# Five shared PSUM banks, more heads in plain F32, and fewer transfers in a fused attention and gated-MLP kernel

## The chip, the cores and the metric

The kernel runs on one core of a Trainium2 chip. Each time is device time in microseconds (us) of one execution. The kernel before was timed three times: 784.73, 786.86 and 790.17 us; the median is 786.86 us. The profile comes from one further execution, which took 793.39 us.

A core has five engines that run side by side and wait for each other through semaphores: TensorE (PE in the profile; its weight loads are a row of their own, PEld), VectorE (DVE), ScalarE (ACT), GpSimd (POOL) and SyncE (SP), which in this kernel issues all the DMAs. TensorE writes into PSUM, eight banks of 128 x 512 F32 values; all else lies in SBUF.

## The reference

Two stages follow each other, for 8 batches of 576 positions. The first is attention with 8 heads of 64 dimensions per batch (64 heads in all); the second is a feed-forward part with a token-mixing gate, which adds its input at the end.

```python
scores = scale * np.matmul(q, k.transpose(0, 1, 3, 2))
cum = np.cumsum(np.maximum(s, 0.0), axis=-1)
bias = -(cum[:, :, :, None] - cum[:, :, None, :])
scores = np.where(causal, -1e9, scores + np.minimum(bias, 0.0))
attn = softmax(scores)                       # max taken off, sum + 1e-9
x = heads_side_by_side(np.matmul(attn, v))   # (8, 576, 512)

h = gelu_tanh(x @ w_in)                      # 512 -> 1024
u, v = h[..., :512], h[..., 512:]
v_n = (v - mean(v)) / np.sqrt(var(v) + 1e-6) * g_ln
v_s = np.einsum('ts,bsd->btd', w_sg, v_n) + b_sg[None, :, None]   # mixes positions
out = x + (u * v_s) @ w_out
```

In each row of scores the term of the query's own running sum is a constant, so only the key's running sum is added: a row of the running sum stands beside the key's 64 rows, and a row of ones beside the query's.

## The kernel before, in words

**Two ways to multiply.** TensorE takes plain F32, or F32R, a shortened F32. Most products are made in F32R from split operands: a value is copied as F32R (the high part), what is lost is taken off (`x - high`, the low part), and the products high x high, high x low and low x high are summed in PSUM. `split` (lines 590-597) makes the two parts, most often the high one on ACT and the low one on POOL or DVE. The first heads avoid splits: up to `NQ` (8) the scores, and up to `NP` (12) the sums of probabilities and values, are plain F32 products. In the profile an F32 product has two records.

**Scores of one head** (`scores`, lines 852-881). The 576 queries are five tiles, the keys are only taken up to the diagonal, so six products of 448, 64, 320, 192, 288 and 288 columns fill four PSUM banks. `qk_part` (799-807) makes one product in F32, or two in F32R. DVE adds the causal mask and finds the row's extreme (`ttr`), ACT takes the exponential and its sum (`exp_`). A scores bank is free again when DVE has read it. `transposes` (883-944) turns the probabilities on TensorE and copies or splits them out of PSUM; `pv` (946-1013) multiplies them with V. Every second head, `scales` and `spread_scales` send the inverse sums through DRAM and a broadcast.

**Operands of a head.** `load` (609-629) fetches a plain head's key and query as two blocks of 128 rows (64 of data, one of ones, 63 of zeros) and then puts the running sum in row 64 of the key's block. For a later head it fetches one raw block; `split_head` (781-797) splits it and moves the halves about with four SBUF copies and one transfer from DRAM (`k<-cum`). The first copy of a running-sum row (head 0) is also the gate behind which the loads under `later()` are issued: the weights of the feed-forward part and the raw blocks.

**Feed-forward part of one batch** (`ffn`, lines 1016-1160): 5 units `v` (into `vm`), 8 units `u` (`um`), 8 units `s` (`sm`, token mixing with the bias) and 8 units `o` (`om`), each with 8 to 14 products in one PSUM bank, followed by a series on ACT, DVE and POOL. It runs beside the attention of the next batch. The weights are prepared once, during the first two batches: `w_in` and `w_out` by a series on ACT, POOL and DVE per piece (`part`), the token weights by `w_sg_part` (744-769) from half tiles `wst` in the eight-buffer ring `u2`. The token bias goes as high and low part into rows 64 and 65 of `wr2`, by transfers.

**PSUM.** Four pools: scores two banks (`ps_sc`, line 582), transposes two, sums one, feed-forward three (`ps_m`, line 585). In the last batch, the feed-forward part draws on all but the sums' bank in turn (`rings`, line 1019). A pool's banks are given to its tiles in the order in which the tiles are written in the program.

**The order of the work.** The program is not written in the order in which it runs. Each step is placed at a time counted in heads (`POS`, `place`, `spread`), and each instruction gets that time as its priority, shifted by a table `SHIFT` per kind of instruction and phase. `plan` (437-560) then goes through a model of the engines with costs (`cost`, the table `FULL` for plain F32 products, `MARGIN`, `ISSUE`) and fixes for every engine the sequence in which it takes its instructions. Each engine runs its sequence strictly in that order. Eight products that nobody reads (`WARM`, tile `wm`, lines 656-658) stand before the first head.

All instructions go through one helper, so the profile has them all on line 418; groups are told apart by the names of their tiles.

Of the kernel before, what the change touches and what calls it, by code (L numbers as in the profile page):

```python
# [71 lines left out]
MARGIN = 54.24  # L72
ISSUE = 550.0
PHASE = (4.0, 9.0, 13.5, 61.5)
SHIFT = {
    "act activation p__ 128x192 p__": (3.011, -1.887, 0, 0, 0),
    "act activation p__ 128x576 p__": (-3.548, 0, 0, 0, 0),
# [3 lines left out]
    "act activation wbits 128x256 wraw": (-0.436, -0.436, -0.436, -0.436, 0),  # L81
    "act copy k 128x576 raw": (0, 4.274, 4.274, 4.274, 4.274),
    "act copy pah 128x512 pt": (0, 0, 1.072, 4.27, 0),
    "act copy pal 128x512 pt": (0, 0, 4.218, 0, 0),
    "act copy pbh 128x256 pt": (2.434, 2.434, 2.434, 2.434, 2.434),
    "act copy pbl 128x256 pt": (1.753, 1.753, 1.753, 0, 0),
    "act copy vs 128x384 vr": (0, 0, 1.645, 0, 0),
    "act copy wi 128x256 wbits": (1.607, 0, 0, 0, 0),
# [9 lines left out]
    "dve scalar_tensor_tensor wbits 128x256 wraw": (1.384, 1.384, 1.384, 1.384, 0),  # L98
    "dve scalar_tensor_tensor wm 128x256 wraw": (11.665, 0, 0, 0, 0),
    "dve tensor_copy pbl 128x512 pt": (2.602, 2.602, 2.602, 0, 0),  # L100
    "dve tensor_scalar wm 128x256 wbits": (-1.597, 3.567, 0, 0, 0),
    "dve tensor_tensor pbl 128x512 pt": (0, 0, 0, 5.115, 0),
    "dve tensor_tensor_reduce p__ 128x192 sc": (0, 0, 3.283, 0, 0),
    "dve tensor_tensor_reduce p__ 128x288 sc": (-1.373, 0, 0, 0, 0),
    "dve tensor_tensor_reduce p__ 128x320 sc": (6.772, 0, 6.985, 5.285, 0),
    "dve tensor_tensor_reduce p__ 128x448 sc": (-0.88, 0, 0, 0, 0),
    "dve tensor_tensor_reduce p__ 64x64 sc": (-11.268, -11.268, -11.268, -11.268, -11.268),
# [25 lines left out]
    "pool tensor_scalar p__ 64x64 p__": (0, 2.769, 0, 0, 0),  # L133
    "pool tensor_scalar wbits 128x256 wbits": (0, -2.08, 0, 0, 0),
    "pool tensor_tensor bh 1x288 wst": (0, 0, 4.905, 0, 0),
    "pool tensor_tensor vn 128x512 vt": (0, 0, -3.713, -3.713, -3.713),
    "pool tensor_tensor wo 128x256 wbits": (0, 0, 10.618, 10.618, 0),
    "pool tensor_tensor ws 128x288 wst": (0, 0, -1.463, 0, 0),
# [425 lines left out]
def tile_attn_gmlp(  # L564
    ctx: ExitStack,
    tc: tile.TileContext,
    kq: bass.AP,
    vp: bass.AP,
# [40 lines left out]
    def load(h):  # L609
        d = heads[h] = {}  # L610
        if h < NQ:
            k = d["k"] = att.tile([P, S], F32, name="kf", tag="k1")
            q = d["q"] = att.tile([P, S], F32, name="qf", tag="q1")
            nc.sync.dma_start(out=k, in_=kq[h, 0:P])
            nc.sync.dma_start(out=q, in_=kq[h, D:D + P])
            x = nc.sync.dma_start(out=k[D:D + 1, :], in_=cf[h:h + 1, :])
            if h == 0:
                first.append(x)
        else:
            d["raw"] = att.tile([P, S], F32, name="raw", tag="raw", bufs=1)  # L620
# [123 lines left out]
    def w_sg_part():  # L744
        with later():
            nc.sync.dma_start(out=g_b, in_=g_ln.rearrange("(o d) -> o d", o=1).broadcast_to([P, DH]))
        for j in range(NT):
# [7 lines left out]
        for f in range(2):
            fs = slice(f * CH, f * CH + CH)
            t = moe.tile([P, CH], F32, name="wst", tag="u2", bufs=U2)
            nc.sync.dma_start(out=t[0:REM, :], in_=w_sgt[NT * P:S, fs])
            nc.sync.dma_start(out=t[REM:P, :], in_=w_sgt[NT * P:S, fs])
            nc.scalar.copy(out=wr1[:, fs], in_=t)  # L760
# [508 lines left out]
```

## Time and profile before

| | |
|---|---|
| median of three executions | 786.86 us (784.73 to 790.17) |
| the profiled execution | 793.39 us, of which 791.7 us from the first to the last instruction |
| TensorE busy | 770.2 us (97%) |
| weight loads busy | 693.9 us (88%) |
| DVE, ACT, POOL busy | 602.8, 569.0, 497.6 us |
| data moved by DMA | 98.93 MB in 75567 packets |
| mean granted TensorE clock | 0.989 |

A row of the groups reads: line, engine, operation, output tile <- input tiles, the shape of one, its count | the time in which at least one of them ran (us), the mean of one (ns) | idle time of the engine before them and what ended it. A row of the stretches gives, from A to B us, the stretch's length, each engine's busy time with its count of instructions, the granted clock of TensorE as a share of full speed, and the DMA engines' busy share and GB/s. A row of the waits: engine and tile that waited <- engine and tile that ended it: us in total, times, longest. A row of the chain or of the timeline: start, length, what. TensorE's records overlap, since a matmul's record lasts from its issue to the end of its last result.

### The profile page before, as it was taken

To read this page: it belongs to the slowest core of one execution; us is meant where nothing else is said; L and a number is where in the kernel's file an instruction comes from. 1 tells how busy PE (TensorE), PEld (TensorE's weight loads), DVE (VectorE), ACT (ScalarE), POOL (GpSimd) and SP (SyncE) were. 2 spreads that over 40 slices of the span, in tenths; PEclk is the share of its full clock that TensorE was granted. 3 is DMA by queue.
4 is the path that set the end of the run, shared out by engine and by line. 5 is a ranking of instruction groups with operands and counts; after the bars stand their busy time and mean duration, and the time that the engine had idled before them with its cause. 6 is when DMAs were issued, how large, how long until landed. Compare 5 with 4: busy or idle time off the path is not lost.

```text
span 791.7 us, 16950 instructions
## 1 busy us (share of the span) xinstructions
PE 770.2 (97%) x5225; PEld 693.9 (88%) x5225; DVE 602.8 (76%) x1849; ACT 569.0 (72%) x1576; POOL 497.6 (63%) x775
## 2 busy tenths in 40 slices
PE   7999899999999999999999999999999999999998
PEld 5566667999989998999999998999989999999998
DVE  5884678877797688976798767976889767984562
ACT  4786667977688677886788776886788867882340
POOL 4588777667577566675566575775576756663632
PEclk9999889999999999999999999999999999999999
DMA  7777653465535553555444635355544555310101
GB/s 219 206 228 189 186 125 97 120 165 131 142 84 142 131 140 102 133 133 140 131 119 104 165 94 141 91 138 132 142 110 117 135 147 131 95 33 31 59 8 61
DMA packets 75567, 98.93 MB, mean 125 GB/s; under 512 B 27298, under 2 KB 43876, under 8 KB 75476
## 3 DMA queue, kind: packets, MB, share of 16 engines
q1 hardware_dynamic: 75476, 97.84, 46.3%
q8 instruction: 42, 0.69, 0.4%
q14 instruction: 49, 0.40, 0.2%
HBM read 51.71 MB, written 9.90 MB: 78 GB/s over the span
## 4 chain that ended last, share of the span: by engine, by line
PE 75%; DVE 10%; DMA 5%; POOL 3%; issue 3%; ACT 2%; SPq 1%; POOLq 0%; DVEq 0%; ACTq 0%
PE sm L418 12%; PE om L418 12%; PE vm L418 11%; PE sc L418 11%; PE xx L418 9%; PE pt L418 9%; PE um L418 9%; DVE p L418 3%; DMA k<-k 2%; DMA rb<-rd 2%; SPq L418 1%; DVE u L418 1%; POOL k L418 1%; DVE vm L418 1%; DVE bs L418 1%
## 5 line engine op out<-in xcount | busy, mean ns | idle before, releaser
L418 ACT ACTIVATE p<-p,mn 128x192 f32<-128x192 f32 (+4 forms) x320 | 177.6, 556 | 38.2 <-DVE mn L418 36.3
L418 PE MATMUL sc<-k,q 128*128 128x288 f32 (+9 forms) x672 | 142.0, 310 | 5.5 <-DMA k<-k 2.6
L418 DVE CUSTOM_DVE_ANT_0 p<-sc,mask 128x448 f32<-128x448 f32 (+4 forms) x320 | 123.0, 421 | 25.9 <-PE sc L418 24.1
L418 PE MATMUL pt<-ident,p 128*128 128x128 f32 x768 | 132.0, 279 | 4.2 <-ACT p L418 1.5
L418 PE MATMUL sm<-ws,vn 128*128 128x288 f32 x768 | 134.0, 303 | 0.0
L418 PE MATMUL um<-xs,wi 128*128 128x288 f32 x768 | 127.4, 302 | 1.3 <-DVE u L418 1.3
L418 PE MATMUL om<-gt,wo 128*128 128x288 f32 x768 | 128.2, 299 | 0.0
L418 PE MATMUL vm<-wi,xs 128*128 128x512 f32 (+1 forms) x416 | 122.7, 409 | 0.3 <-POOL xs L418 0.2
L418 PEld LDWEIGHTS sc<-k,q 128*128 128x128 f32 (+3 forms) x672 | 104.0, 183 | 19.4 <-DVE mn L418 4.2
L418 PEld LDWEIGHTS pt<-ident,p 128*128 128x128 f32 x768 | 92.3, 141 | 21.3 <-issue 3.4
L418 PEld LDWEIGHTS um<-xs,wi 128*128 128x128 f32 x768 | 108.4, 188 | 2.9 <-DVE u L418 1.9
L418 PEld LDWEIGHTS sm<-ws,vn 128*128 128x128 f32 x768 | 110.4, 189 | 0.6 <-DVE u L418 0.2
L418 PEld LDWEIGHTS om<-gt,wo 128*128 128x128 f32 x768 | 110.2, 188 | 0.6
L418 POOL TENSOR_TENSOR k<-raw,k 128x576 fp32r<-128x576 f32 x56 | 79.9, 1426 | 11.6 <-ACT k L418 7.9
L418 POOL TENSOR_TENSOR gt<-u,gt 128x288 fp32r<-128x288 f32 x64 | 50.6, 807 | 54.8 <-ACT gt L418 54.5
L418 PEld LDWEIGHTS vm<-wi,xs 128*128 128x128 f32 (+1 forms) x416 | 72.9, 186 | 12.8 <-POOL xs L418 1.2
L418 POOL TENSOR_TENSOR vs<-vr,vs 128x384 fp32r<-128x384 f32 x52 | 52.7, 1013 | 39.7 <-ACT vs L418 33.0
L418 POOL TENSOR_TENSOR xr<-xr,rb 128x576 f32<-128x576 f32 x32 | 45.7, 1428 | 50.4 <-DMA rb<-rd 38.2
L418 DVE SCALAR_TENSOR_TENSOR u<-u,um 128x288 f32<-128x288 f32 x128 | 55.6, 442 | 9.4 <-ACT u L418 8.8
L418 DVE TENSOR_TENSOR pbl<-pt,pbh 128x512 fp32r<-128x512 f32 x104 | 56.1, 546 | 7.4 <-ACT pbh L418 6.9
L418 ACT ACTIVATION_READ_ACCUMULATOR p<-p,mn 128x1 f32 (+1 forms) x320 | 60.3, 188 | 0.0
L418 ACT CAST pbh<-pt 128x512 fp32r<-128x512 f32 x104 | 49.5, 477 | 8.8 <-PE pt L418 7.3
(126 smaller groups left out, 1562.7 us busy)
## 6 DMA issues: line engine op xcount, KB each, us to landing
q<-k SPq DMA_DIRECT2D x168, 144.0 KB
raw<-in_kq SPq DMA_DIRECT2D x56, 288.0 KB
vr<-in_vp SPq DMA_DIRECT2D x52, 192.0 KB
rb<-rd SPq DMA_DIRECT2D x64, 144.0 KB
out_t<-ot SPq DMA_DIRECT2D x64, 144.0 KB
k<-k SPq DMA_DIRECT2D x56, 144.0 KB
wraw<-in_w_in SPq DMA_DIRECT2D x16, 256.0 KB
vf<-in_vp SPq DMA_DIRECT2D x12, 192.0 KB
```

What stands on the lines that cost most here:

```text
L418: r = getattr(op["eng"].real, op["name"])(*[f(a) for a in op["args"]], **{k: f(v) for k, v in op["kw"].items()})
```

## The change

- **PSUM.** `ps_m` has five banks and `ps_sc` is another name for it: scores tiles take the tag of the feed-forward tiles. The running sum's first products (`cps`) take their bank from the transposes' pool. The last batch's turn of banks names `ps_m` where it named `ps_sc`.
- **Plain F32.** `NQ` goes from 8 to 12 and `NP` from 12 to 16: scores of heads 8 to 11, and sums of heads 12 to 15, need no splits.
- **Loads of plain heads.** A new input `kf` holds, for these twelve heads, 65 rows (64 of data, one of ones) with key and query side by side. One load brings both into one tile `[P, 2, S]`; the products read 65 rows. The running-sum row still follows, except for head 0. Split heads use the same tile for `k1` and `q1`.
- **Head 0.** Its six scores products read 64 rows, and each gets a second F32 product of one row: a row of ones (`tri[0:1]`) times the running sum where it lies (`cf[0:1]`). The gate for `later()` is now head 0's load of V.
- **Token weights and bias.** Four whole tiles in place of eight halves, taken from the four-buffer ring `gt`; two loads in place of four for the last 64 positions; the bias is loaded once, into partition 64, and split straight into rows 64 and 96 of `wr2`, with zeros between. The four transfers `wr<-bh` are gone. `wr2` and `vnr2` have 97 rows in place of 66.
- **Order.** `WARM` goes from 8 to 2, `MARGIN`, `ISSUE` and `FULL` have other values, and the `SHIFT` table is replaced, so that each engine's sequence is a new one.

```diff
-WARM = 8
+WARM = 2
...
-NQ = 8
-NP = 12
+NQ = 12
+NP = 16
...
-MARGIN = 54.24
-ISSUE = 550.0
+MARGIN = 33.09
+ISSUE = 640.0
...
-    ps_sc = Pool(ctx.enter_context(tc.tile_pool(name="ps_sc", bufs=2, space=bass.MemoryType.PSUM)), "ps_sc", 2, psum=True)
...
-    ps_m = Pool(ctx.enter_context(tc.tile_pool(name="ps_m", bufs=3, space=bass.MemoryType.PSUM)), "ps_m", 3, psum=True)
+    ps_m = Pool(ctx.enter_context(tc.tile_pool(name="ps_m", bufs=5, space=bass.MemoryType.PSUM)), "ps_m", 5, psum=True)
+    ps_sc = ps_m
...
-            k = d["k"] = att.tile([P, S], F32, name="kf", tag="k1")
-            q = d["q"] = att.tile([P, S], F32, name="qf", tag="q1")
-            nc.sync.dma_start(out=k, in_=kq[h, 0:P])
-            nc.sync.dma_start(out=q, in_=kq[h, D:D + P])
-            x = nc.sync.dma_start(out=k[D:D + 1, :], in_=cf[h:h + 1, :])
-            if h == 0:
-                first.append(x)
+            t = att.tile([P, 2, S], F32, name="kf", tag="k1")
+            k, q = d["k"], d["q"] = t[0:D + 1, 0, :], t[0:D + 1, 1, :]
+            nc.sync.dma_start(out=t[0:D + 1], in_=kf[h])
+            if h:
+                nc.sync.dma_start(out=k[D:D + 1, :], in_=cf[h:h + 1, :])
...
-            nc.sync.dma_start(out=d["v"], in_=vp[h])
+            x = nc.sync.dma_start(out=d["v"], in_=vp[h])
+            if h == 0:
+                first.append(x)
...
+    one = tri[0:1].bitcast(F32)
...
-        ps = ps_sc.tile([P, 512], F32, name="cps", tag="sc")
+        ps = ps_pt.tile([P, 512], F32, name="cps", tag="pt")
...
-    wr2 = const.tile([66, S], F32R, name="wr2")
-    vnr2 = const.tile([66, DH], F32R, name="vnr2")
-    nc.vector.memset(vnr2[64:66, :].bitcast(F32), 1.0)
+    wr2 = const.tile([97, S], F32R, name="wr2")
+    vnr2 = const.tile([97, DH], F32R, name="vnr2")
+    nc.vector.memset(vnr2[64:97, :].bitcast(F32), 1.0)
+    nc.gpsimd.memset(wr2[64:96, :].bitcast(F32), 0.0)
...
-            for f in range(2):
-                fs = slice(f * CH, f * CH + CH)
-                t = moe.tile([P, CH], F32, name="wst", tag="u2", bufs=U2)
-                with later():
-                    nc.sync.dma_start(out=t, in_=w_sgt[j * P:(j + 1) * P, fs])
-                split(ws[:, j, 0, fs], ws[:, j, 1, fs], t, *eng("ws"))
-                yield 1
...
+            t = moe.tile([P, S], F32, name="wst", tag="gt", bufs=4)
+            with later():
+                nc.sync.dma_start(out=t, in_=w_sgt[j * P:(j + 1) * P])
+            split(ws[:, j, 0], ws[:, j, 1], t, *eng("ws"))
+            yield 2
...
-            split(bh[:, 0, :], bh[:, 1, :], t[0:1, :], nc.scalar, eng("ws1")[0])
-            nc.sync.dma_start(out=wr2[64:65, fs].bitcast(F32), in_=bh[:, 0, :].bitcast(F32))
-            nc.sync.dma_start(out=wr2[65:66, fs].bitcast(F32), in_=bh[:, 1, :].bitcast(F32))
...
+        nc.sync.dma_start(out=t[64:65], in_=b_sg.rearrange("(o t) -> o t", o=1))
+        split(wr2[64:65], wr2[96:97], t[64:65], nc.scalar, eng("ws1")[0])
...
+        if h == 0:
+            nc.tensor.matmul(o, d["q"][0:D, i0:i0 + r], d["k"][0:D, j0:j1], start=True, stop=False)
+            nc.tensor.matmul(o, one[:, 0:r], cf[0:1, j0:j1], start=False, stop=True)
+            return
...
-        t = ps_sc.tile([P, 512], F32, name="sc", tag="sc")
+        t = ps_sc.tile([P, 512], F32, name="sc", tag="m")
```

The last edit stands four times in `scores`. Besides, the 73 entries of `SHIFT` are replaced by 59 others, `kq` loses its rows of ones and zeros, and `kf` is laid out on the host from the same data.

More of the change, by code (lines that the diff above doesn't have):

```diff
@@ L47 @@
 CV = 1.4
-WARM = 8
-FULL = {(128, 192): 300.0, (128, 288): 525.0, (128, 320): 690.0, (128, 448): 830.0, (64, 64): 230.0,
-        (64, 128): 140.0, (64, 192): 205.0, (64, 256): 265.0}
-NQ = 8
-NP = 12
+WARM = 2
+FULL = {(128, 192): 300.0, (128, 288): 525.0, (128, 320): 690.0, (128, 448): 830.0, (64, 64): 130.0,
+        (64, 128): 150.0, (64, 192): 215.0, (64, 256): 290.0}
+NQ = 12
+NP = 16
 U2 = 8
@@ L71 @@
 YIELD = {DVE: 95, POOL: 60}
-MARGIN = 54.24
-ISSUE = 550.0
+MARGIN = 33.09
+ISSUE = 640.0
 PHASE = (4.0, 9.0, 13.5, 61.5)
 SHIFT = {
-    "act activation p__ 128x192 p__": (3.011, -1.887, 0, 0, 0),
-    "act activation p__ 128x576 p__": (-3.548, 0, 0, 0, 0),
[3 rows of a table removed]
[L81 to L88, printed above, removed]
[9 rows of a table removed]
[L98 to L107, printed above, removed]
[25 rows of a table removed]
[L133 to L138, printed above, removed]
[10 rows of a table removed]
@@ new lines @@
+    "act activation p__ 128x192 p__": (0, -1.37, 0, 0, 0),
+    "act activation p__ 128x320 p__": (-2.28, -2.28, -2.28, -2.28, -2.28),
+    "act activation p__ 64x64 p__": (2.65, 0, -4.17, 0, 0),
[3 rows of a table added]
+    "act copy k 128x576 raw": (0, 0, 6.86, 6.86, 6.86),
+    "act copy pah 128x512 pt": (3.74, 3.74, 3.74, 3.74, 3.74),
+    "act copy pbh 128x256 pt": (0, 2.82, 1.23, 0, 0),
+    "act copy vs 128x384 vr": (0, 0, 0, 5.9, 0),
+    "act copy wi 128x256 wbits": (1.22, 1.22, 1.22, 0, 0),
+    "act copy wo 128x256 wbits": (0, 0, -0.77, -0.77, 0),
[8 rows of a table added]
@@ new lines @@
+    "dve scalar_tensor_tensor wbits 128x256 wraw": (0, 0.25, 4.43, 0, 0),
+    "dve scalar_tensor_tensor wm 128x256 wraw": (0, -5.7, 0, 0, 0),
+    "dve tensor_copy pbl 128x512 pt": (0, 0, -2.8, 0, 0),
+    "dve tensor_copy pdh 128x256 pt": (-3.99, -3.99, -3.99, -3.99, 0),
+    "dve tensor_scalar wm 128x256 wbits": (1.21, 1.21, 1.21, 0, 0),
+    "dve tensor_tensor pdh 64x64 pt": (0, 0, 0, 2.01, 2.01),
+    "dve tensor_tensor xr 64x64 x": (0, 0, 0, 5.88, 5.88),
+    "dve tensor_tensor_reduce p__ 128x192 sc": (-3.17, -3.17, -3.17, -3.17, -3.17),
@@ new lines @@
+    "dve tensor_tensor_reduce p__ 128x288 sc": (0, 0.71, 4.68, 0, 0),
+    "dve tensor_tensor_reduce p__ 128x320 sc": (4.12, 0.53, 8.43, 1.82, 0),
+    "dve tensor_tensor_reduce p__ 64x64 sc": (-9.27, -9.27, -9.27, -9.27, -9.27),
[18 rows of a table added]
+    "pool tensor_scalar wbits 128x256 wbits": (-4.38, -4.38, -4.38, -4.38, 0),
+    "pool tensor_tensor k 128x576 raw": (0, 0, -8.31, -8.31, -8.31),
+    "pool tensor_tensor wo 128x256 wbits": (0, 0, 19.21, 19.21, 0),
+    "pool tensor_tensor ws 128x576 wst": (0, 0, -3.49, 0, 0),
[6 rows of a table added]
@@ L567, in tile_attn_gmlp @@
     kq: bass.AP,
+    kf: bass.AP,
     vp: bass.AP,
@@ L621, in load @@
             with later():
-                nc.sync.dma_start(out=d["raw"], in_=kq[h, 0:2 * D])
+                nc.sync.dma_start(out=d["raw"], in_=kq[h])
         if h < NP:
             d["v"] = att.tile([P, 6, 2, D], F32, name="vf", tag="vs")[:, :, 0, :]
-            nc.sync.dma_start(out=d["v"], in_=vp[h])
+            x = nc.sync.dma_start(out=d["v"], in_=vp[h])
+            if h == 0:
+                first.append(x)
         else:
@@ L747, in w_sg_part @@
         for j in range(NT):
-            for f in range(2):
-                fs = slice(f * CH, f * CH + CH)
-                t = moe.tile([P, CH], F32, name="wst", tag="u2", bufs=U2)
-                with later():
-                    nc.sync.dma_start(out=t, in_=w_sgt[j * P:(j + 1) * P, fs])
-                split(ws[:, j, 0, fs], ws[:, j, 1, fs], t, *eng("ws"))
-                yield 1
[L755 to L760, printed above, removed]
-            eng("ws1")[0].tensor_tensor(out=wr2[0:REM, fs], in0=t[0:REM, :], in1=wr1[0:REM, fs].bitcast(F32),
-                                    op=ALU.subtract)
-            t = moe.tile([P, CH], F32, name="wst", tag="u2", bufs=U2)
-            bh = moe.tile([1, 2, CH], F32R, name="bh", tag="gt", bufs=4)
-            nc.sync.dma_start(out=t[0:1, :], in_=b_sg.rearrange("(o t) -> o t", o=1)[:, fs])
-            split(bh[:, 0, :], bh[:, 1, :], t[0:1, :], nc.scalar, eng("ws1")[0])
-            nc.sync.dma_start(out=wr2[64:65, fs].bitcast(F32), in_=bh[:, 0, :].bitcast(F32))
-            nc.sync.dma_start(out=wr2[65:66, fs].bitcast(F32), in_=bh[:, 1, :].bitcast(F32))
-            yield 1
+            t = moe.tile([P, S], F32, name="wst", tag="gt", bufs=4)
[3 more added lines that the diff above has]
+            yield 2
+        t = moe.tile([P, S], F32, name="wst", tag="gt", bufs=4)
+        nc.sync.dma_start(out=t[0:REM, :], in_=w_sgt[NT * P:S])
+        nc.sync.dma_start(out=t[REM:P, :], in_=w_sgt[NT * P:S])
+        nc.scalar.copy(out=wr1, in_=t)
+        eng("ws1")[0].tensor_tensor(out=wr2[0:REM], in0=t[0:REM], in1=wr1[0:REM].bitcast(F32), op=ALU.subtract)
+        yield 1
+        t = moe.tile([P, S], F32, name="wst", tag="gt", bufs=4)
+        nc.sync.dma_start(out=t[64:65], in_=b_sg.rearrange("(o t) -> o t", o=1))
+        split(wr2[64:65], wr2[96:97], t[64:65], nc.scalar, eng("ws1")[0])
+        yield 1
     def w_out_part():
@@ L784, in split_head @@
             raw = d["raw"]
-            k1 = att.tile([P, S], F32R, name="k1", tag="k1")
+            t = att.tile([P, 2, S], F32R, name="k1", tag="k1")
+            k1, q1 = t[:, 0, :], t[:, 1, :]
             k2 = att.tile([P, S], F32R, name="k2", tag="k2")
-            q1 = att.tile([P, S], F32R, name="q1", tag="q1")
             d["k1"], d["k2"], d["q1"] = k1, k2, q1
@@ L862, in scores @@
         yield 0.5
-        t = ps_sc.tile([P, 512], F32, name="sc", tag="sc")
+        t = ps_sc.tile([P, 512], F32, name="sc", tag="m")
         qk_part(h, 2, t, 0, 0, 320)
@@ L870, in scores @@
         yield 0.5
-        t = ps_sc.tile([P, 512], F32, name="sc", tag="sc")
+        t = ps_sc.tile([P, 512], F32, name="sc", tag="m")
         qk_part(h, 4, t, 0, 0, CH)
         ttr(h, 4, t, 0, 0, CH, True)
-        t = ps_sc.tile([P, 512], F32, name="sc", tag="sc")
+        t = ps_sc.tile([P, 512], F32, name="sc", tag="m")
         qk_part(h, 4, t, 0, CH, S)
@@ L1216, in tile_attn_gmlp @@
     nc.emit(tc, new, uses, seqs, nc.eager(pre, new, uses, order, bufs, seqs, after))
-_INS = ["kq", "vp", "s_t", "w_in", "g_ln", "w_sgt", "b_sg", "w_out"]
+_INS = ["kq", "kf", "vp", "s_t", "w_in", "g_ln", "w_sgt", "b_sg", "w_out"]
 def _layout(i):
@@ L1228, in _layout @@
     tok = (np.array(TOK)[:, None] * REM + np.arange(REM)).ravel()
-    pad = np.zeros((BH, D, S), q.dtype)
-    pad[:, 0] = 1
-    kq = np.concatenate([k.transpose(0, 2, 1), q.transpose(0, 2, 1)[:, :, tok], pad], axis=1)
+    kq = np.concatenate([k.transpose(0, 2, 1), q.transpose(0, 2, 1)[:, :, tok]], axis=1)
+    kf = kq[:NQ].reshape(NQ, 2, D, S).transpose(0, 2, 1, 3)
+    kf = np.concatenate([kf, np.ones((NQ, 1, 2, S), q.dtype)], axis=1)
     v6 = np.concatenate([v, v[:, NT * P:], v[:, 0:REM], v[:, 0:REM]], axis=1)
@@ L1239, in _layout @@
         "kq": kq,
+        "kf": kf,
         "vp": v6.reshape(BH, 6, P, D).transpose(0, 2, 1, 3),
```

2 lines of the change are left out of this document (1 added, 1 removed), and 82 rows, old and new, of the table SHIFT.

## The prediction

> **What bounds the kernel now.** I read the page's first part, then the table of busy time by stretches, then TensorE's waits, then the chain of waits where that table shows holes, and last the groups that the edits touch.
>
> ```profile
> span 791.7 us, 16950 instructions
> PE 770.2 (97%) x5225; PEld 693.9 (88%) x5225; DVE 602.8 (76%) x1849; ACT 569.0 (72%) x1576; POOL 497.6 (63%) x775
> ```
>
> TensorE (PE) is the bound of the whole. No other engine is near its limit, so work taken off DVE, ACT, POOL or the DMA queue counts only where PE waits for it. The stretches say where:
>
> ```profile
> core 0: us, PE busy (x) PEld busy (x) DVE busy (x) ACT busy (x) POOL busy (x), PEclk, DMA share, GB/s
> 140.00:720.00 580.00, 575.42 (x4039) 540.28 (x4039) 467.38 (x1445) 451.13 (x1241) 368.32 (x563) 1.00 0.47 122
> 80.00:140.00 60.00, 53.77 (x312) 40.61 (x310) 46.77 (x137) 42.67 (x121) 45.84 (x75) 0.89 0.53 136
> 20.00:30.00 10.00, 8.54 (x50) 5.06 (x49) 7.40 (x24) 6.30 (x21) 5.30 (x9) 0.83 0.68 214
> ```
>
> From 140 to 720 us, attention of one batch beside the feed-forward part of the batch before it, PE is idle 580 - 575.42 = 4.6 us at full clock: little to win. From 80 to 140 us, where heads 8 to 15 meet the first feed-forward part and the last of the weight preparation, PE is idle 60 - 53.77 = 6.2 us, and its granted clock is 0.89: 53.77 x 0.11 = 5.9 us of work lost to the slower clock. From 20 to 30 us it is 1.5 us idle and 8.54 x 0.17 = 1.5 us slow. These four, 15.1 us, are the pool that the change can draw on. What PE waits for:
>
> ```profile
> PE cps L418 <- DVE sp L418: 5.1, 1, 5.1
> PE sc L418 <- DMA k<-k: 2.6, 3, 1.9
> PE sc L418 <- DVE mn L418: 1.8, 4, 0.8
> PE um L418 <- DVE u L418: 1.3, 5, 0.3
> ```
>
> The first is the start. The second is a scores matmul waiting for a copy inside a split key; the chain of waits shows what stands before it:
>
> ```profile
> 78.49 1.89 DMA wr<-bh
> ...
> 81.57 0.57 ACT k L418
> ...
> 82.27 1.42 POOL k L418
> 83.69 0.81 POOL wbits L418
> ...
> 90.06 4.73 DMA k<-k
> 94.79 0.14 issue
> 94.93 1.14 PE sc L418 x3
> ```
>
> A split on ACT, its rest on POOL, weight pieces on POOL and a queue of issues on SP (84.50 to 90.06), a copy that lands after 4.73 us, and only then the scores. The bias transfer for the token weights stands in the same chain. This is what the change takes away for heads 8 to 11.
>
> **The change part by part.**
>
> *F32 scores for heads 8 to 11* (NQ 8 to 12). Each loses one copy on ACT, one subtraction on POOL, four SBUF copies and one row from DRAM; it gets a load and one row. PE pays:
>
> ```profile
> L418 PE MATMUL sc<-k,q 128*128 128x288 f32 (+9 forms) x672 | 142.0, 310 | 5.5 <-DMA k<-k 2.6 <-DVE mn L418 1.8 <-issue 1.0
> L418 PE MATMUL sc<-kf,qf 128*128 128x288 f32 (+4 forms) x96 | 31.1, 427 | 0.0
> ```
>
> Split heads: 142.0 / 56 = 2.54 us of PE each. F32 heads: 31.1 / 8 = 3.89 us (an F32 product has two records, so twelve per head either way). Difference 1.35 us, four heads: +5.4 us. The load of 65 rows in place of two of 128 halves the bytes; PE's list has no scores wait for such a load, so that is worth nothing by itself.
>
> *F32 sums for heads 12 to 15* (NP 12 to 16). The stretch rows of the two kinds, filtered by V's tile:
>
> ```profile
> 28.00:60.00 32.00, 9.62 (x80) 5.64 (x80) 0.99 0.73 214
> 200.00:300.00 100.00, 18.21 (x89) 1.00 0.48 128
> ```
>
> F32: 20 records per head, 9.62 / 4 = 2.41 us. Split: 10 records per head, 18.21 / 8.9 = 2.05 us. Difference 0.36 us, four heads: +1.4 us. Both figures carry the pipeline's tail; if the tail is the larger part in the split kind, the true price is up to double, +2.8. These heads' sums lie around 140 us, from where on PE is the bound, so nothing hides this. ACT, DVE and POOL drop the splits of V, of the transposed probabilities and of the result.
>
> *What the splits' absence gives back.* Of the 12.1 us lost in 80 to 140 I take 10 as regained: the holes at the scores go, the fuller PE keeps its clock, and the SP queue sheds the four bias-row copies, half of the token-weight loads and the split heads' copies. Head 12 is the first split head now and its copies are issued after the weights are through, so the late chain shortens there as well. Of the 3 us at 20 to 30 I take 0.5. Sum -10.5; the ends are 0 (the holes belong to the feed-forward start and move to the next wait) and -15.1.
>
> For the clock, the row says 0.83 in 20 to 30 us although PE was busy 8.54 of those 10 us. The Trainium skill, "TensorE: Matmul & The Clock Gate", section "HAM oscillation — how this bites in real kernels", gives as its abstract rule no PE idle gaps above about 3.4 us. No gap of 3.4 us fits into 1.5 us of idle time, so the trace disagrees: shorter holes cost clock here. By the page's rule no hole in this stage would throttle, the clock's share (7.4 us) could not be regained by closing holes, and the sum would be 10.5 / 15.1 of 7.4, or 5.1 us, worse: 784.8 us; by the row it stands.
>
> *Start.* These are timeline rows of SP and PE:
>
> ```profile
> 1.23 0.67 SPq L418 DMA_DIRECT2D vf<-in_vp  x1
> 7.61 3.78 PE L418 MATMUL wm<-tri,sp 128*128 128x512 f32 x8
> 8.20 0.62 SPq L418 DMA_DIRECT2D kf<-cf  x1
> 8.87 0.58 SPq L418 DMA_DIRECT2D wraw<-in_w_in  x1
> 11.19 3.21 PE L418 MATMUL sc<-kf,qf 128*128 128x448 f32 x10
> ```
>
> Six warm-up products fewer free 6 / 8 x 3.78 = 2.8 us, and head 0 no longer waits for the row copied at 8.20. But its six products get six one-row F32 partners, and no row shows a one-row product. The nearest show that rows hardly count:
>
> ```profile
> L418 PE MATMUL sc<-k,q 128*128 128x288 f32 x112 | 34.7, 312 | 0.7 <-DVE mn L418 0.6
> L418 PE MATMUL sc<-k,q 66*128 66x288 f32 x112 | 33.3, 299 | 0.0
> ```
>
> So the partners may cost as much as head 0's own scores, 3.9 us, were PE always busy then. They run while the softmax of head 0 starts, and the first scores can start 2.8 us sooner. I take 0; the ends are -2.8 and +3.9. PE's queue is in order, so head 0's partners wait for the running sum with all of head 0 behind them; the sum is ready at 8.20, before PE gets there. The gate that held weight loads back until 8.87 now hangs on V's first load, issued at 1.23 here. Preparation can begin some 5 us earlier; PE is busy with attention meanwhile, so I take -0.5.
>
> *Token weights.* Four whole tiles in place of eight halves, in the four-buffer ring that raw weights and gated tiles share: fewer issues, but a queue for buffers. The first user is the first `sm` product, in the chain at 137.93 us, so this costs nothing; uncovered, a buffer would be late by one POOL split.
>
> ```profile
> 137.93 1.39 PE sm L418 x9
> ```
>
> *Five shared PSUM banks.* Waits of scores for `mn` (1.8) and of `um` for `u` (1.3) are, as I read them, waits for a bank: at most -3.1. I take -1.5; the other sign is a rival below.
>
> *New order.* It can win the 4.6 us idle after 140 us, or lose as much. I take -1.5.
>
> Sum: +5.4 + 1.4 - 10.5 + 0 - 0.5 - 1.5 - 1.5 = -7.2 us. The profiled span becomes 784.5 us, its own time 793.39 - 7.2 = 786.2. That execution lies 6.5 us above the median shown, 786.86, so I carry the difference over: 786.9 - 7.2 = **779.7 us**.
>
> **The rivals.**
>
> *A shared ring that blocks (slower).* Banks of a ring are granted in the written order, so a scores tile now stands behind feed-forward tiles. A `vm` tile holds its bank over this series:
>
> ```profile
> L418 ACT ACTIVATE vt<-vm 128x512 f32<-128x512 f32 x32 | 19.0, 595 | 16.4 <-PE vm L418 15.6 <-POOL bs L418 0.4
> L418 DVE SCALAR_TENSOR_TENSOR vt<-vt,vm 128x512 f32<-128x512 f32 x32 | 21.7, 682 | 14.1 <-ACT vt L418 14.1
> L418 ACT ACTIVATE vt<-vt 128x512 f32<-128x512 f32 x32 | 20.1, 631 | 8.3 <-DVE vt L418 8.3
> L418 DVE SCALAR_TENSOR_TENSOR vm<-vt,vm 128x512 f32<-128x512 f32 x32 | 22.0, 688 | 5.9 <-ACT vt L418 5.9
> L418 DVE BATCH_NORM_STATS2 bs<-vm 128x6 f32<-128x512 f32 x32 | 22.1, 691 | 0.2
> L418 DVE BATCH_NORM_AGGREGATE bs<-bs 128x2 f32<-128x6 f32 x32 | 5.5, 172 | 0.2
> L418 DVE SCALAR_TENSOR_TENSOR vt<-vm,bs,g_b 128x512 f32<-128x512 f32 x32 | 23.7, 744 | 0.5
> 118.48 1.79 PE um L418 x12
> ```
>
> 595 + 682 + 631 + 688 + 691 + 172 + 744 = 4.2 us. If one such hold per batch stops PE, with one unit's twelve matmuls (1.79) to cover it, that is 2.4 us in seven batches, +16.9: 796.6 us. It decides from (794.7 - 779.7) / 7 = 2.1 us per batch on. For it: all tiles of both streams now pass one queue. Against it: waits for a bank are small today with three and two.
>
> *The holes stay (within 1%).* PE gets the 6.8 us of F32 work, and only 3 us come back because ACT, DVE and POOL chains of the first feed-forward part take the place of the key's: 790.7 us. For it: PE's list names DVE's `mn` beside the copy.
>
> *Order and banks give all (faster).* The whole pool of 15.1, 4.6 after 140 us and 2.8 at the start against 6.8: -15.7, 771.2 us. For it speaks that the loads of weights filled only 540.28 of 580 us. The Trainium skill, "Perfetto Trace Analysis", section "Identifying the Most-Contended Engine", calls that row, not matmul busy time, the measure of headroom; by it 39.7 us could be left, and the sum would have room far below 771. The trace bears it out only in part, as a weight load of a 512-column product is shorter than the product.
>
> *Nothing done by the fewer transfers.* True after 140 us already (DMA share 0.47); it is in the sum.
>
> **How the numbers follow.** A measurement of this kernel tells about 1% from no change: below 779.0 is faster, above 794.7 slower. Forecast 0.50, split by its nearness to 779.0 into 0.23 faster and 0.27 same; all given 0.22, faster; holes stay 0.17, same; ring blocks 0.11, slower. So 0.45, 0.44, 0.11. The forecast's own range is 773 to 786. For 8 in 10 it reaches down past 771.2 to 768 (the banks' 3.1 on top) and up to 791, the holes' case; left out are the ring and the outer tail.
>
> **What would show it.** Right: PE idle in 80 to 140 us below 3 us and its clock near 1.00; no scores wait for `k<-k` before 100 us; `sc<-kf` groups of 12 heads at 3.9 us each. Wrong: idle over 1.5 us per 100 us after 140 us with `mn` or `vt` as releaser (ring), or the clock still below 0.95 at 80 to 140 us (holes stay), or a first `sc` later than 11.2 us.

## The result, and the profile after

| | before | after |
|---|---|---|
| median of four executions | 786.95 us (784.73 to 790.17) | 796.74 us (795.80 to 798.65) |
| ratio, with its 95% interval | 1 | 1.0124 (1.0084 to 1.0164) |
| the profiled execution, and its span | 793.39, 791.7 us | 795.80, 794.1 us |

The changed kernel is 1.2% slower. A fourth execution of before, 787.05 us, ran beside after and moves its median to 786.95. The two profiled executions lie only 2.4 us apart, since the profiled one of before is slower than all four that were timed, and the one of after is the fastest of its own four: the traces show less of the loss than the medians. Four executions of the experiments below, one of e1 (822.57 us), one of e3 (799.60) and two of e12 (1895 and 2595), fell into a slower state of the chip and count in no median, ratio or range.

The first part of the page of after, and the row of the granted clock from its second part (40 equal slices):

```profile
span 794.1 us, 16905 instructions
PE 782.0 (98%) x5271; PEld 692.7 (87%) x5271; DVE 599.1 (75%) x1829; ACT 562.6 (71%) x1550; POOL 488.0 (61%) x762
PEclk9999999999999999999999999999999999999999
```

TensorE is busy 11.8 us longer than before, DVE, ACT and POOL less long. The row of the granted clock shows nothing amiss. The same stretches as in the prediction, for after:

```profile
core 0: us, PE busy (x) PEld busy (x) DVE busy (x) ACT busy (x) POOL busy (x), PEclk, DMA share, GB/s
20.00:30.00 10.00, 10.00 (x29) 5.50 (x28) 4.80 (x17) 4.12 (x13) 2.77 (x5) 1.00 0.21 56
80.00:140.00 60.00, 57.50 (x351) 39.59 (x352) 48.43 (x146) 43.93 (x129) 48.55 (x71) 1.00 0.63 166
140.00:720.00 580.00, 579.19 (x4084) 541.57 (x4084) 468.41 (x1443) 454.71 (x1242) 375.29 (x578) 1.00 0.46 122
```

From 80 to 140 us, PE's idle time fell from 6.2 to 2.5 us and the clock rose from 0.89 to 1.00. From 140 to 720 us, idle time fell from 4.6 to 0.8 us. Both stages gained, as predicted. From 20 to 30 us, PE is busy all the time, but it issues 29 products, where before had 50 in 8.54 us. TensorE's waits no longer have the copy inside the key (`k<-k`) nor `mn`; these are the first, second and fifth of the list:

```profile
PE sc L404 <- DMA kf<-in_kf: 4.9, 1, 4.9
PE sc L404 <- DMA kf<-cf: 1.0, 1, 1.0
...
PE um L404 <- DVE vt L404: 0.3, 1, 0.3
```

So the loss is no wait. It is in how long a product takes. TensorE's timeline of after (start, length, operation, shape, count):

```profile
4.87 1.85 PE L404 MATMUL sc<-kf 64*128 64x448 f32 x2 [4.87 <-DMA kf<-in_kf]
...
9.22 1.16 PE L404 MATMUL wm<-tri,sp 128*128 128x512 f32 x2
...
12.64 1.86 PE L404 MATMUL sc<-cf,tri 1*128 1x448 f32 x2
...
23.04 2.11 PE L404 MATMUL sc<-kf 65*128 65x448 f32 x4
...
28.67 1.12 PE L404 MATMUL pt<-ident,p 128*128 128x128 f32 x4
...
36.27 1.02 PE L404 MATMUL sc<-kf 65*128 65x448 f32 x2
```

and two rows of the same timeline of before:

```profile
15.29 1.02 PE L418 MATMUL sc<-kf,qf 128*128 128x448 f32 x2
...
19.13 0.66 PE L418 MATMUL pt<-ident,p 128*128 128x128 f32 x4
```

Two records of 448 columns take 1.02 us at full clock, before and after, with 128 rows or 65. At 4.87 and 12.64 us in after, two take 1.85 and 1.86; at 28.67 us four transposes take 1.12 where before needs 0.66. After runs at half clock until some 35 us: its first full-clock record in the trace is at 35.5 us, that of before at 11.8. The column of the granted clock reads 1.00 up to the first such record, so it hid this. Half clock for 35.5 - 11.8 = 23.7 us longer loses about 11.8 us of work. That is more than the slowdown, and as much as PE's extra busy time; the other terms of that, 6.8 us of F32 work added (the prediction's price) and 7.4 us of slow clock gone in the two stages that the prediction priced, nearly cancel.

The list of groups shows it too, when its busy time is divided by the heads:

```profile
L404 PE MATMUL sc<-kf 65*128 65x448 f32 (+8 forms) x144 | 49.5, 453 | 6.7 <-DMA kf<-in_kf 4.9 <-DMA kf<-cf 1.0 <-DVE xr L404 0.9
L404 PE MATMUL sc<-cf,tri 1*128 1x288 f32 (+4 forms) x12 | 7.0, 704 | 0.0
```

The plain scores take 49.5 / 12 = 4.1 us per head, and head 0's twelve records of one row 7.0 us; in before, a head's plain scores took 3.9.

### The profile page after: what moved, and what is told of

Its sections match the earlier page's. It is cut to its first block, busy times and chain, and to the rows that moved or that the text cites. A ratio compares the mean times of both kernels' runs of the same rounds, so it can differ in the third digit from the quotient of the medians.

```text
span 794.1 us, 16905 instructions
## 1 busy us (share of the span) xinstructions
PE 782.0 (98%) x5271; PEld 692.7 (87%) x5271; DVE 599.1 (75%) x1829; ACT 562.6 (71%) x1550; POOL 488.0 (61%) x762
## 4 chain that ended last, share of the span: by engine, by line
PE 93%; DVE 2%; DMA 2%; ACT 2%; POOL 0%; issue 0%; SPq 0%; ACTq 0%
PE sc L404 16%; PE sm L404 14%; PE om L404 13%; PE um L404 13%; PE xx L404 13%; PE vm L404 12%; PE pt L404 11%; DMA wraw<-in_w_out 1%; ACT p L404 1%; DMA kf<-in_kf 0%; DVE wbits L404 0%; DVE p L404 0%; DMA k<-k 0%; PE cps L404 0%; PE x L404 0%
## 5 line engine op out<-in xcount | busy, mean ns | idle before, releaser
L404 ACT ACTIVATE p<-p,mn 64x64 f32<-64x64 f32 (+4 forms) x320 | 177.8, 556 | 58.9 <-DVE mn L404 56.9
L404 PE MATMUL om<-gt,wo 128*128 128x288 f32 x768 | 129.8, 301 | 0.0
L404 PE MATMUL vm<-wi,xs 128*128 128x512 f32 (+1 forms) x416 | 117.6, 404 | 0.0
L404 PEld LDWEIGHTS sm<-ws,vn 128*128 128x128 f32 x768 | 112.6, 188 | 1.2 <-issue 0.3
L404 PEld LDWEIGHTS um<-xs,wi 128*128 128x128 f32 x768 | 107.6, 188 | 3.3 <-issue 0.8
L404 POOL TENSOR_TENSOR k<-raw,k 128x576 fp32r<-128x576 f32 x52 | 74.7, 1437 | 32.4 <-ACT k L404 30.9
L404 PE MATMUL sc<-k 128*128 128x288 f32 (+4 forms) x312 | 91.2, 304 | 0.0
L404 PE MATMUL sc<-k,q 66*128 66x288 f32 (+4 forms) x312 | 86.8, 307 | 0.0
L404 POOL TENSOR_SCALAR p<-p 64x64 f32<-64x64 f32 x128 | 30.9, 241 | 81.0 <-ACT p L404 50.5
L404 DVE TENSOR_TENSOR pbl<-pt,pbh 128x512 fp32r<-128x512 f32 x96 | 52.0, 547 | 23.1 <-ACT pbh L404 20.2
L404 DVE SCALAR_TENSOR_TENSOR u<-u,um 128x288 f32<-128x288 f32 x128 | 56.4, 445 | 10.1 <-ACT u L404 9.7
L404 POOL TENSOR_TENSOR vs<-vr,vs 128x384 fp32r<-128x384 f32 x48 | 48.7, 1015 | 18.8 <-ACT vs L404 17.7
```

The costliest lines, as they stand in the source:

```text
L404: r = getattr(op["eng"].real, op["name"])(*[f(a) for a in op["args"]], **{k: f(v) for k, v in op["kw"].items()})
```

## The experiments

Two theories of why the clock comes late. **W:** the eight warm-up products released it; two are too few. **R:** products that use few rows of the array do not count as work for the clock; head 0's partners use one row, its scores 64 and the plain heads 65, where before all used 128. The rivals from the prediction, the ring and the order, come after that. All kernels compute the whole result; padding is rows of zeros.

### More warm-ups, more rows: four kernels

**e1**: after with eight warm-up products; the six more cost nothing in the planner, so that the order all but stays.

```diff
-WARM = 2
+WARM = 8
```

> The changed kernel with eight warm-up products in place of two, its order otherwise kept. In the changed kernel TensorE runs at half clock until 35.5 us, before the change until 11.8 us. Theory W (the number of warm-up products decides): full clock from about 12 us on, as before the change, 24 us at full instead of half clock, less 2.8 us for the products: about 786 us. Theory R (the clock follows how many of the 128 operand rows the products use; head 0's one-row and 64-row products and the other plain heads' 65-row products count for little): full clock may come near 12 us, but the one-row stretch takes it away again until after 30 us: 792 to 797 us.

**e2**: after, with the plain scores read over 128 rows (63 of them zeros; 64 for head 0), order kept. Head 0's partners keep their one row.

```diff
-            k, q = d["k"], d["q"] = t[0:D + 1, 0, :], t[0:D + 1, 1, :]
-            nc.sync.dma_start(out=t[0:D + 1], in_=kf[h])
+            k, q = d["k"], d["q"] = t[:, 0, :], t[:, 1, :]
+            nc.sync.dma_start(out=t, in_=kf[h])
...
-            nc.tensor.matmul(o, d["q"][0:D, i0:i0 + r], d["k"][0:D, j0:j1], start=True, stop=False)
+            nc.tensor.matmul(o, d["q"][:, i0:i0 + r], d["k"][:, j0:j1], start=True, stop=False)
```

> The changed kernel with two warm-up products, but the plain heads' key and query padded with zero rows to 128 rows, as before the change; head 0 keeps its one-row products. Theory W: still half clock until about 35 us, 796 us (twice the bytes in the loads, hidden). Theory R: the one-row stretch ends near 22 us, from then on all products have 128 rows, so full clock comes near 25 us in place of 35.5: about 5 us less, 791 to 792 us.

**e3**: before, with its plain scores read over 65 rows, order identical.

```diff
-nc.tensor.matmul(o, d["q"][:, i0:i0 + r], d["k"][:, j0:j1], start=True, stop=True)
+nc.tensor.matmul(o, d["q"][0:D + 1, i0:i0 + r], d["k"][0:D + 1, j0:j1], start=True, stop=True)
```

> The kernel before, same order, but its plain scores products read 65 rows in place of 128 (the rows left out are zeros). Theory W: nothing changes, 787 us, full clock from 11.8 us. Theory R: the clock falls back in the first 60 us, where these products fill a third of TensorE's time, 2 to 8 us more: 789 to 795 us.

**e4**: before with two warm-up products, order kept.

```diff
-WARM = 8
+WARM = 2
```

> The kernel before, same order, with two warm-up products in place of eight. Theory W: half clock until after 25 us, 8 to 12 us more: 795 to 799 us. Theory R: the products that follow have 128 rows, so full clock still comes between 12 and 15 us and the time stays within 2 us of 787.

Measured on one chip, before at 788.34 us there; the last column is the trace's first record of full clock:

| | median us | ratio (95%) | full clock from |
|---|---|---|---|
| e1 after, eight warm-ups | 801.75 | 1.0184 (1.0126 to 1.0242) | 12.5 us, but half again from 15.9 to 50.1 |
| e2 after, scores of 128 rows | 790.19 | 1.0029 (1.0002 to 1.0056) | 28.3 us |
| e3 before, scores of 65 rows | 791.54 | 1.0035 (0.9994 to 1.0076) | 27.2 us |
| e4 before, two warm-ups | 789.96 | 1.0016 (0.9990 to 1.0043) | 15.2 us |

W falls on both sides: six warm-ups fewer cost before next to nothing, and six more do not make after faster; e1 lies above what either theory expected of it. In e1 the clock is released early and lost again, while PE is busy without a gap. The stretch of 20 to 30 us has transitions of the clock on both sides, and the first one lies within 10 to 20 us, so here the clock's column can be read:

```profile
10.00:20.00 10.00, 10.00 (x27) 5.37 (x25) 3.87 (x15) 4.43 (x14) 5.00 (x7) 0.80 0.45 141
20.00:30.00 10.00, 10.00 (x29) 5.50 (x28) 5.04 (x17) 4.31 (x13) 2.52 (x4) 0.50 0.20 56
```

and two rows of its timeline:

```profile
13.84 1.01 PE L406 MATMUL sc<-cf,tri 1*128 1x448 f32 x2
...
28.13 1.12 PE L406 MATMUL pt<-ident,p 128*128 128x128 f32 x4
```

The one-row products start at full clock (1.01 us for two of 448 columns), and within their stretch the clock is halved. The four transposes then take 1.12 us at a granted 0.50; that is the length they have in after at 28.67 us, where the column says 1.00. The stretch of 20 to 30 us also has the same 29 products as after.

In e2 the clock comes 7 us earlier than in after. Its timeline, at the same four transposes:

```profile
23.45 2.11 PE L404 MATMUL sc<-kf 128*128 128x448 f32 x4
...
28.72 0.66 PE L404 MATMUL pt<-ident,p 128*128 128x128 f32 x4
```

In e3 the rows alone move the release from 11.8 to 27.2 us, with eight warm-ups and no one-row product:

```profile
17.64 1.70 PE L418 MATMUL sc<-kf,qf 65*128 65x448 f32 x2
...
24.66 1.12 PE L418 MATMUL pt<-ident,p 128*128 128x128 f32 x4
```

The first is the pair that takes 1.02 us in before. R's mechanism holds in this trace, but its price in time is not clear of noise: e3's ratio has 1 inside its interval. Its nine executions lie from 786.42 to 797.29 us, and in the profiled one 80 to 140 us ran at a clock of 0.94 (0.89 in before). Part of what the start lost came back later; I have no run that says why. Two of the nine recorded a clock of 0.979 and 0.981, and took 797.29 and 796.32 us; none of the 57 executions of before that ran beside the experiments recorded less than 0.988.

### Both kinds of products with all rows

**e5**: e2, and head 0's partners over 128 rows too: a tile with ones in row 0 and zeros elsewhere, times the running sum's tile with its rows 64 to 127 set to zero. Order kept.

```diff
-    one = tri[0:1].bitcast(F32)
+    one = moe.tile([P, S], F32, name="one", tag="xs", bufs=4)
+    nc.gpsimd.memset(one, 0.0)
+    nc.gpsimd.memset(one[0:1], 1.0)
+    nc.gpsimd.memset(cf[BH:P], 0.0)
...
-            nc.tensor.matmul(o, one[:, 0:r], cf[0:1, j0:j1], start=False, stop=True)
+            nc.tensor.matmul(o, one[:, 0:r], cf[:, j0:j1], start=False, stop=True)
```

> The changed kernel with zero rows added so that every plain scores product and head 0's added products read 128 rows; two warm-up products, order kept. Theory R (operand rows decide the clock): full clock between 11 and 16 us in place of 28.3 (the run that padded the scores products alone) and 35.5 (the changed kernel); 13 us at full instead of half clock, so some 6 us less than that run's 790.2: 783 to 785 us. Theory D (what is left is the doubled work of head 0's added products, not the clock): full clock still after 25 us, 789 to 791 us.

**e6**: e5 with eight warm-up products.

```diff
-WARM = 2
+WARM = 8
```

> The same with eight warm-up products. Theory R: the clock comes no earlier, as nothing with few rows runs at the start, and the six products cost at most 2.8 us while TensorE is the bound: 0 to 3 us more than the run with two. If the number of warm-up products counts after all: 2 to 5 us less.

**e9** (run later): after with only e5's change to the partners (its tile of ones and zeros too), the scores left at 64 and 65 rows.

```diff
-nc.tensor.matmul(o, one[:, 0:r], cf[0:1, j0:j1], start=False, stop=True)
+nc.tensor.matmul(o, one[:, 0:r], cf[:, j0:j1], start=False, stop=True)
```

> The changed kernel, order kept, with only head 0's added products padded from one row to 128; head 0's own products keep 64 rows and the other plain heads' 65. Fourth corner beside the changed kernel (neither padded: full clock at 35.5 us, 1.0124 of before), the run with only the scores padded (28.3 us, 1.0029) and the one with both (13.4 us, 0.9968). If rows decide, head 0's stretch is then half full and the 65-row products keep the next windows near 0.7: full clock between 20 and 30 us, 1.002 to 1.007 of before. If the one-row products alone were to blame: near 13 us, 0.997.

| | median us | ratio (95%) | full clock from |
|---|---|---|---|
| e5 scores and partners of 128 rows | 785.33 (before 788.54) | 0.9968 (0.9944 to 0.9992) | 13.4 us |
| e6 the same, eight warm-ups | 785.77 (before 788.54) | 0.9966 (0.9941 to 0.9991) | 13.8 us |
| e9 partners alone | 795.07 (before 787.86) | 1.0067 (1.0030 to 1.0104) | 35.9 us |

The timeline of e5:

```profile
9.67 1.16 PE L406 MATMUL wm<-tri,sp 128*128 128x512 f32 x2
...
12.65 1.31 PE L406 MATMUL sc<-cf,one 128*128 128x448 f32 x2
...
20.80 0.66 PE L406 MATMUL pt<-ident,p 128*128 128x128 f32 x4
...
25.31 1.02 PE L406 MATMUL sc<-kf 128*128 128x448 f32 x2
```

The order is that of after, so rows can be set side by side. From the warm-ups to the pair of 448 columns, after takes 36.27 - 9.22 = 27.05 us, e5 25.31 - 9.67 = 15.64. This stretch alone gives 11.4 us. The two profiled executions differ by 794.1 - 783.4 = 10.7 us, the medians, which were taken beside different runs of before, by 796.74 - 785.33 = 11.4, and the ratios by 1.56%, 12.3 us. So the clock at the start accounts for the whole difference between after and e5, and the rows of zeros, which add nothing to the result, take it back. Warm-ups again do nothing: e6 is e5.

Of the ratios, the scores' rows alone are worth 1.0124 - 1.0029 = 0.95%, the partners' rows alone 0.57%, both 1.56%. The partners alone do not stand clear of the noise, since the intervals of e9 and after overlap; that they matter once the scores are padded follows from e2 and e5, 1.0029 and 0.9968, whose intervals do not. In e9's profiled execution (800.3 us, the longest of ten) the release is no earlier than in after, where 20 to 30 us was expected:

```profile
28.26 1.12 PE L406 MATMUL pt<-ident,p 128*128 128x128 f32 x4
80.00:140.00 60.00, 57.35 (x317) 38.65 (x318) 45.71 (x134) 41.36 (x119) 44.18 (x63) 0.91 0.60 161
```

The clock of 0.91 is a second fall, from 107.6 to 117.9 us, which loses 5.1 us; without it, this execution would lie at e9's median. The other nine lie from 788.86 to 796.4 us, and their start has no trace.

e5 is faster than both kernels, by 0.3% (0.1 to 0.6) against before. Its stretches and its plain scores:

```profile
80.00:140.00 60.00, 58.70 (x380) 42.76 (x378) 50.05 (x147) 46.35 (x133) 50.45 (x75) 1.00 0.59 162
140.00:720.00 580.00, 578.93 (x4074) 542.58 (x4073) 461.35 (x1418) 444.50 (x1215) 369.01 (x566) 1.00 0.45 121
```

```profile
L406 PE MATMUL sc<-kf 128*128 128x448 f32 (+4 forms) x144 | 45.2, 420 | 6.9 <-DMA kf<-in_kf 5.6 <-DMA kf<-cf 1.3
L406 PE MATMUL sc<-cf,one 128*128 128x288 f32 (+4 forms) x12 | 3.9, 432 | 0.0
```

### What the heads, the order and the ring are worth

With the clock mended, e5 is the base for the rest. Each of these changes something that the planner sees, so each has an order of its own; **e8** and **e12** change nothing but that.

**e7**: e5 with eight plain heads, as before.

```diff
-NQ = 12
+NQ = 8
```

> The padded changed kernel with plain F32 scores for 8 heads as before the change, order planned anew. The prediction's step (the splits of heads 8 to 11 make TensorE wait between 80 and 140 us, more than the 5.4 us their F32 products cost): 2 to 6 us more than the padded kernel, idle TensorE and half clock between 80 and 140 us. The other reading (the F32 products are not covered): 2 to 5 us less.

**e8**: e5 with another margin in the planner.

```diff
-MARGIN = 33.09
+MARGIN = 36.0
```

> The padded changed kernel with another margin in the planner (36 for 33.09), nothing else: the sequences differ, the work does not. It measures what a new order alone is worth. If the order is a small term, as the prediction has it (within 4.6 us): within 4 us of the padded kernel. If the order is the larger part of the gain after 140 us: 5 us or more above it.

**e12**: the same, to the other side.

```diff
-MARGIN = 33.09
+MARGIN = 30.0
```

> The padded kernel, shared ring, margin 30: a second order that nobody chose. If the order that came with the change is worth about 1% over such orders: 1.005 to 1.015 of before. If the run with margin 36 was an outlier: within 0.003 of the padded kernel's 0.9968.

**e10**: e5 with two banks for scores and three for the feed-forward units, as before.

```diff
-    ps_m = Pool(ctx.enter_context(tc.tile_pool(name="ps_m", bufs=5, space=bass.MemoryType.PSUM)), "ps_m", 5, psum=True)
-    ps_sc = ps_m
+    ps_sc = Pool(ctx.enter_context(tc.tile_pool(name="ps_sc", bufs=2, space=bass.MemoryType.PSUM)), "ps_sc", 2, psum=True)
+    ps_m = Pool(ctx.enter_context(tc.tile_pool(name="ps_m", bufs=3, space=bass.MemoryType.PSUM)), "ps_m", 3, psum=True)
...
-name="sc", tag="m")
+name="sc", tag="sc")
```

The last edit stands four times in `scores`; besides, the last batch's turn of banks names `ps_sc` again.

> The padded kernel with separate rings again, two banks for scores and three for the feed-forward part, order planned anew. To be read against the shared ring with an order planned anew (margin 36: 1.0104 of before). If sharing is worth something: 1.013 or more. If sharing costs (the ring rival): below 1.007. If it makes no difference beside the order: 1.007 to 1.013.

**e11**: e10 with the margin of e8.

```diff
-MARGIN = 33.09
+MARGIN = 36.0
```

> Separate rings as in the run before, with margin 36: the same work as the shared ring with margin 36, so the pair differs by the rings and by the order that follows. Sharing worth something: over 1.013 here too; sharing costs: below 1.007 here too; if one of the pairs goes each way, the order outweighs the rings.

| | median us | ratio to before (95%) |
|---|---|---|
| e5, the base | 785.33 | 0.9968 (0.9944 to 0.9992) |
| e8 margin 36 | 795.62 | 1.0104 (1.0046 to 1.0161) |
| e12 margin 30 | 797.21 (two executions) | 1.0111 (1.0029 to 1.0193) |
| e7 eight plain heads | 798.84 | 1.0144 (1.0096 to 1.0193) |
| e10 two rings | 812.36 | 1.0309 (1.0247 to 1.0370) |
| e11 two rings, margin 36 | 809.39 | 1.0258 (1.0190 to 1.0326) |

**The order.** A new margin to either side, with nothing else changed, costs 1.4% (1.0104 and 1.0111 against 0.9968), some 11 us. e8 and e12 from 140 to 720 us:

```profile
140.00:720.00 580.00, 575.38 (x4005) 534.70 (x4004) 458.93 (x1408) 443.16 (x1209) 364.12 (x562) 1.00 0.45 120
```

```profile
140.00:720.00 580.00, 576.89 (x4021) 533.76 (x4019) 464.82 (x1422) 446.86 (x1219) 366.91 (x570) 1.00 0.45 120
```

e8 is idle 4.6 us there, e5 1.1. But e8 also issued 69 products fewer in the same 580 us; at 580 / 4074 = 0.142 us each that is 9.8 us, of which the idle time explains 3.5. The rest is lost while PE shows as busy. In the traces I took the time from each product's start to the next one's, against the median in e5 for products of the same shape. By this e8 loses some 10 us more than e5 in the stage: 5.1 in pauses of over 0.3 us (12 of them with 6.2 us, 2 with 1.1 in e5), 4.6 in pauses of 0.05 to 0.3 us (37.1 us against 32.5). So the new order brings more short pauses, and a good part of them lies under the record of the product before, which still counts as busy. What each pause waits for is not settled.

**The heads.** e7's stage of 80 to 140 us has the hole of before again; the other rows are TensorE's three longest waits there:

```profile
80.00:140.00 60.00, 54.02 (x330) 40.44 (x327) 43.02 (x130) 41.17 (x118) 47.92 (x69) 0.90 0.71 180
PE pt L406 <- POOL p L406: 2.3, 1, 2.3
PE um L406 <- DVE mn L406: 1.8, 1, 1.8
PE sc L406 <- DMA k<-k: 0.7, 1, 0.7
```

Idle 6.0 us and 54.02 x 0.10 = 5.4 us slow, 11.4 in all, against 1.3 in e5; e12 with its own new order has 3.7 idle and no slow clock there, e8 0.8. So the hole goes with the heads' splits. The copy inside the key that the prediction named ends 0.7 us of the waits; the longer two end with other work of POOL and DVE, so which part of the splits makes the hole is not shown. In the whole time, e7 is 13.5 us above e5, where 2 to 6 were expected, and only some 0.35% (2.8 us) above e8 and e12, which is within their intervals. It saves the F32 products of four heads, and its own order also loses less after 140 us (4049 products there, 4005 in e8); the runs do not separate the two.

**The ring.** e10 and e11 have idle time after 140 us, 11.2 and 11.3 us (e10's trace has no transition of the clock, so its 1.00 says nothing):

```profile
140.00:720.00 580.00, 568.79 (x3934) 524.26 (x3931) 449.27 (x1386) 431.55 (x1190) 350.50 (x548) 1.00 0.44 118
```

```profile
140.00:720.00 580.00, 568.73 (x3942) 527.03 (x3942) 449.11 (x1385) 432.66 (x1191) 353.93 (x548) 1.00 0.44 118
```

and e10's second and third waits of TensorE are, read as the prediction read them, those for a bank:

```profile
PE sc L406 <- DVE mn L406: 4.6, 5, 2.5
PE um L406 <- DVE u L406: 3.9, 8, 0.9
```

4.4 us of these two waits lie after 140 us (3.6 and 0.8). By the pauses of over 0.3 us, counted as above, e10 and e11 lose 14.9 us each in the stage, e8 6.2 and e12 3.5. Against e8 and e12, which also have orders that nobody chose, two rings cost 1.5 to 2%. The comparison has a bias: the table of shifts was made for the shared ring. Nor can ring and order be added onto before, which has an order of its own for its two rings; no neighbour of that one was run.

## Why the prediction was wrong

The forecast was 779.7 us with a range to 791; it measured 796.74, in the case "slower", which had a chance of 0.11.

**The step that failed: the start.** "I take 0; the ends are -2.8 and +3.9." It cost 11.4 us. It failed in two ways. It priced the one-row products by the nearest duration rows and read from them that "rows hardly count". For the length of one product that is right: two records of 448 columns take 1.02 us with 128 rows and with 65, and 1.01 with one. But the rows decide when and whether the clock is granted, and through it the length of every product around them, until 35.5 us. And it did not ask at all what the edit from 128 to 65 rows does in the plain heads' scores; it counted their bytes only. Its own terms stayed within its bounds: the twelve records of partners take 3.9 us in e5, the upper end, and the warm-ups are worth nothing.

**The paragraph on the clock.** The prediction read from one row that holes shorter than 3.4 us slow the clock, and stopped at holes. Holes alone do not decide it: before is idle 1.5 us from 20 to 30 us and falls to half clock at 25.4, e11 is idle 1.6 us from 30 to 40 us (longest 1.1) and its trace has full clock from 12.3 to 131.8. The Trainium skill's "TensorE: Matmul & The Clock Gate" has, in the section "What's actually happening", the clock follow how busy TensorE is, and makes the warm-up a matter of time rather than of a number of products. On the number the runs agree (e4, e6). On being busy they do not: after has PE busy in all of 20 to 30 us and stays at half clock, and e1 loses the clock in a stretch without idle time.

**The F32 scores** came out as priced once the clock was mended: 45.2 / 12 = 3.77 us per head in e5, 3.89 predicted. **What the splits' absence gives back** was right that the hole goes with the splits (e7 brings it back) and right in the stage: 2.5 us are lost in 80 to 140 us in after, so 9.6 of 12.1 came back; I took 10. **The token weights** at nothing: TensorE's waits of after have no `sm` among them. **The F32 sums**, priced at 2.41 us per head, take 7.49 us for 60 records, 2.50 us per head, in e5 from 100 to 140 us. **The weight gate** opens earlier as foreseen, the first load of `w_in` is issued at 3.66 us in after and at 8.87 in before; what that is worth was not taken apart.

**The shared banks** (-1.5, at most 3.1) were sized by the waits of before, probably too small; 1.5 to 2%, 12 to 16 us, is what their absence costs in e10 and e11, under new orders and with the bias named above, so the size stays open. **The new order** (-1.5, at most 4.6 either way) was bounded by the idle time alone; e8 and e12 show 11 us, most of it in pauses that do not count as idle.

**The sum**, with the clock mended: in the profiled executions, e5 is 783.4 - 791.7 = -8.3 us, -7.2 predicted. That the two agree confirms no single term of it, since banks and order were not separated. In medians it is only 785.33 - 788.54 = -3.2. Here a second step failed, "I carry the difference over" from the profiled execution to the median. Over the 57 executions of before that ran beside the experiments, the time goes with the recorded clock: 24 at 0.988 to 0.991 have a mean of 790.3 us, 18 at 0.993 of 788.0, 15 at 0.995 to 0.998 of 786.1. The profiled execution had 0.989 and took 793.39. So its pool held clock that the median execution does not lose, some 790.3 - 788.0 = 2.3 us; the 3.1 us by which it lies above its own group are not explained.

**The rivals.** The ring that blocks gave 796.6 us, and 796.74 was measured; that they are so near is chance, since the cause is another: no scores wait for `mn` or `vt` after 140 us, `um` waits 0.3 us for `vt` once, and two rings are the slower ones. The holes did not stay. That order and banks give all came true for the idle time from 140 to 720 us (0.8 of 4.6 us left), but not for its 771.2 us. **What would show it**: of the signs of "right" those on idle time, clock and `k<-k` came, and the 3.9 us for the scores only in e5 (4.1 in after); those of "wrong" did not. They looked at waits, and at a clock column that says 1.00 in the stretch that was half as fast.

## What to carry to other kernels

Where an edit narrows the rows that F32 products read, or adds products of one row, ask about the clock and not only about the products' own length; rows of zeros may be cheaper than the narrow product. Judge the clock at the start by the length of the same shape early and late, since the column has nothing to say before the first transition. And before an edit that makes a planner run anew is judged, run the planner anew with nothing else changed: here that alone moved the time by 1.4%.

## What the runs showed of the hardware

- A TensorE that is busy all the time, largely with products of one to 65 rows, is not granted the full clock (after, until 35.5 us), and can lose it (e1, at 15.9 us). The same products padded with rows of zeros are: 13.4 us in e5. The number of rows read counts, whatever is in them.
- Once the clock is full, 65-row scores mixed with 128-row transposes can keep it: after has no slow stretch behind 36 us in its profiled execution. They need not: e9 and e1, with the same scores, fall to half clock from 107.6 to 117.9 and from 87.6 to 94.4 us, with 2.7 and 2.9 us idle from 80 to 140 us, where after has 2.5. What decides it there is not known.
- Where the threshold lies stays open. Weighting products by their rows over the 3.4 us ahead of a release (the shortest stretch of half clock in the trace of before, 25.4 to 28.8 us, has this length), I find shares from 0.84 (e3) to 1.0 of 128 rows (before, after, e1, e2), but also stretches of 0.95 (e3, 6.7 to 10.1 us) and 0.92 (e1, 33 to 36 us) that released nothing. The one-row stretch of after has 0.14 to 0.21. In e9 the shares are 0.66 to 0.89 from 12 to 32.5 us, and 1.0 in the 3.4 us ahead of its release at 35.9.
- Busy time of TensorE is no measure of its work: after's 782.0 us and e5's 770.8 us hold the same 5271 products, e5's with more rows.
